# Attention's norms, maxima and denominators: from two-input VectorE steps to one-input sums over neighbouring columns

## The chip, the core and the metric

One Trainium2 chip, one of its cores. The time is the device time of one execution in microseconds (us), the median of several runs. The engines named below are TensorE (PE, with its weight loads PEld), VectorE (DVE), ScalarE (ACT), GpSimd (POOL) and SyncE (SP, which here only starts transfers). Each works through its own list of instructions in order and waits on semaphores for the others.

## The reference, cut to what matters

```python
# attention by random features; batch 4, heads 8, seq 576, head_dim 64, 128 features
q_s, k_s = q * 64**-0.25, k * 64**-0.25
def phi(x):
    proj = einsum('bhsd,md->bhsm', x, omega)
    sq = sum(x * x, -1) / 2.0
    h = proj - sq
    h = h - max(h, -1)
    return exp(h) / sqrt(128)
q_p, k_p = phi(q_s), phi(k_s)
kv = einsum('bhsm,bhsd->bhmd', k_p, v);  z = sum(k_p, 2)
num = einsum('bhsm,bhmd->bhsd', q_p, kv)
den = einsum('bhsm,bhm->bhs', q_p, z)[..., None] + 1e-06
x = num / den                       # (2304 tokens, 512)
# then a top-1 mixture of 8 experts (512 -> 1024 -> 512, ReLU), then an MLP 512 -> 2048 -> 512
```

In exact arithmetic `sq` drops out of `h - max(h)`. The kernel keeps it, so that its rounding follows the reference's.

## The kernel before, in words

The program has three stages: attention with the router (about the first 175 us), the experts, and the last MLP. The change touches the first alone.

Attention works on blocks of 256 tokens of one batch (or of 64 tokens of two batches), 20 for q and k together, and on 36 units: one unit is 4 pairs of heads of a block. For a block, its raw values are squared (`square`: ACT for k, POOL for q), POOL folds the 64 squares of a head into 16 (`tree`, two additions), and DVE sums the 16 (`total`, L449) into `nsq`, one number for each token and head. For a unit, PE transposes (L472), ACT copies (L477), PE projects (L484) into two PSUM banks, DVE takes the maximum over the features of each bank (`top`, L491, into `mx`), DVE forms the exponent's bias in two small steps on 128x8 numbers (`bias`: L495 writes mx = nsq * SQ + mx, L496 writes bi = nsq * SQ - mx, with SQ = -1/16), and ACT takes eight exponentials with that bias (`exps`, L500). k's exponentials go into the sums over tokens (L526), q's are transposed (L584), copied (L588 by ACT, L590 by DVE) and multiplied with those sums (L601). ACT copies the result, 73 columns a head, into `nx` (`copy_out`, L604): 64 numerators, 1 denominator, 8 router logits. DVE adds the epsilon to the denominator (`den`, L612), inverts it (L615), scales the logits (L618) and sums them over the heads (L622). The router's own steps on DVE follow (L657 to L691), and POOL scales the rows that are stored for the experts (L691, `xr`).

The order of the work on all engines is written by a planner (`Plan.run`): each step is added with an engine, a cost, a rank and what it comes after, and the planner's list is the order in which the instructions stand in each engine's queue. DVE and POOL are each one such queue: whatever is late there holds up all that stands behind it. DVE also carries work that belongs to the later stages, such as the second halves of the expert weights (`wl`, L290), and POOL the first halves (L281).

Of the kernel before, what the change touches and what calls it, by code (L numbers as in the profile page):

```python
# [8 lines left out]
F32 = mybir.dt.float32  # L9
# [4 lines left out]
AF = mybir.ActivationFunctionType  # L14
ALU = mybir.AluOpType
AX = mybir.AxisListType.X
# [3 lines left out]
P = 128  # L20
B, H, S, HD = 4, 8, 576, 64
# [6 lines left out]
HV = HD + 1  # L28
HZ = HD + 9
# [3 lines left out]
EPS = 1e-06 * 128.0  # L33
SCALE = float(HD) ** -0.25
SQ = -1.0 / 16.0
# [4 lines left out]
class Plan:  # L40
# [19 lines left out]
    def buf(self, ring):  # L60
        return {"ring": ring, "uses": 0, "end": 0.0}
# [100 lines left out]
def kernel(  # L162
# [14 lines left out]
    nc = tc.nc  # L177
# [146 lines left out]
    with ExitStack() as actx:  # L324
        ap = actx.enter_context(tc.tile_pool(name="ap", bufs=2))
# [3 lines left out]
        def ring(n, shape, name, dtype=F32, pool=ac):  # L329
            return [pool.tile(shape, dtype, name=f"{name}{i}") for i in range(n)]  # L330

        plan = Plan({
            "ps": ring(8, [P, 4, P], "ps", pool=psp),
            "blk": ring(7, [P, 2 * H, HD], "blk"),
            "sqt": ring(2, [P, 2 * H, HD], "sqt"),
            "th": ring(4, [P, 4, P], "th"),
            "pp": ring(11, [P, H, P], "pp"),
            "qt": ring(4, [P, 4, P], "qt"),
            "nx": ring(4, [P, H, HZ], "nx"),
            "xr": ring(3, [P, H, HD], "xr"),  # L340
            "kvc": ring(1, [P, 4, HD], "kvc"),
            "kvt": ring(1, [P, 2, P], "kvt"),
# [2 lines left out]
        add, buf, at = plan.add, plan.buf, plan.tile  # L345
# [11 lines left out]
            nc.gpsimd.memset(tv[:, :, HD:HV], 1.0)  # L357
        for t in kvz:
            nc.gpsimd.memset(t[:, H * HZ:], 0.0)

        def load_v(b):
            t = vmain[b % 2]
# [52 lines left out]
        dve, act, pool = nc.vector, nc.scalar, nc.gpsimd  # L415


        def block_tasks(which, blk, rank):
            src = q if which == "q" else k
            small = blk[0] == "s"  # L420
            n = H if small else 2 * H
            o = {"buf": buf("blk")}

            def load():
                t = at(o["buf"])
                if small:
                    for i in range(2):
                        nc.sync.dma_start(out=t[64 * i:64 * i + 64, 0:H, :],
                                          in_=src[2 * blk[1] + i, :, 512:576, :].rearrange("h p d -> p h d"))
                else:  # L430
                    b, i = blk
                    nc.sync.dma_start(out=t.rearrange("p (h r) d -> p h r d", r=2),
                                      in_=src[b, :, i * 256:(i + 1) * 256, :].rearrange("h (p r) d -> p h r d", r=2))

            def square(eng):
                raw, t = at(o["buf"])[:, 0:n, :], at(sb)[:, 0:n, :]
                if eng == "ACT":
                    act.activation(t, raw, AF.Square)
                else:
                    pool.tensor_mul(t, raw, raw)  # L440

            def tree():
                t = at(sb)[:, 0:n, :]
                for w in (32, 16):
                    pool.tensor_add(t[:, :, 0:w], t[:, :, 0:w], t[:, :, w:2 * w])

            def total():
                o["nsq"] = ap.tile([P, 2 * H], F32, name="nsq", tag="nsq", bufs=12)
                dve.reduce_sum(o["nsq"][:, 0:n], at(sb)[:, 0:n, 0:16], axis=AX)  # L449

            f = 0.5 if small else 1.0
            sb = buf("sqt")
            o["load"] = add("SP", 2250 * f, load, rank - 8, take=[o["buf"]])
            if which == "k":
                t = add("ACT", 950 * f, lambda: square("ACT"), rank - 0.5, after=[o["load"]], take=[sb], use=[o["buf"]])
            else:
                t = add("POOL", 1900 * f, lambda: square("POOL"), rank - 0.5, after=[o["load"]], take=[sb],
                        use=[o["buf"]])
            t = add("POOL", 2000 * f, tree, rank - 0.4, after=[t], use=[sb])
            o["sq"] = add("DVE", 60 + 270 * f, total, rank - 0.3, after=[t], use=[sb])  # L460
            return o

        def unit_tasks(u, o, rank, prev):
            which, blk, hf = u
            r = {}
            ptb, thb, ppb = buf("ps"), buf("th"), buf("pp")

            def turn():  # L470
                for c in range(4):
                    nc.tensor.transpose(at(ptb)[:, c, :],  # L472
                                        at(o["buf"]).rearrange("p a d -> p (a d)")[:, (4 * hf + c) * P:(4 * hf + c + 1) * P],
                                        ident)

            def copy():
                act.activation(at(thb), at(ptb), AF.Copy)  # L477

            def project(c):
                for w in HALVES:
                    for i in range(2):
                        nc.tensor.matmul(at(pjb[i])[w, c, :], lhsT=at(thb)[HALVES[i], c, w], rhs=oms[HALVES[i], :],  # L484
                                         start=True, stop=True)

            def top(i):
                if i == 0:
                    for name in ("mx", "bi"):
                        r[name] = ap.tile([P, 2, 4], F32, name=name, tag=name, bufs=6)  # L490
                dve.reduce_max(r["mx"][:, i, :], at(pjb[i]), axis=AX)  # L491

            def bias():
                sq = o["nsq"][:, 8 * hf:8 * hf + 8].rearrange("p (j i) -> p i j", i=2)
                dve.scalar_tensor_tensor(out=r["mx"], in0=sq, scalar=SQ, in1=r["mx"], op0=ALU.mult, op1=ALU.add)  # L495
                dve.scalar_tensor_tensor(out=r["bi"], in0=sq, scalar=SQ, in1=r["mx"], op0=ALU.mult, op1=ALU.subtract)  # L496

            def exps(i):
                for j in range(4):
                    act.activation(at(ppb)[:, 2 * j + i, :], at(pjb[i])[:, j, :], AF.Exp, bias=r["bi"][:, i, j:j + 1])  # L500

            pjb = [buf("ps"), buf("ps")]
            ta = add("PE", 435, turn, rank - 1.5, after=[o["load"]] + prev, take=[ptb], use=[o["buf"], ptb], mode="whole")
            x = add("ACT", 480, copy, rank - 2.4, after=[ta], take=[thb], use=[ptb])
            for c in range(4):
                x = add("PE", 220, lambda c=c: project(c), rank + 1 + 0.1 * c, after=[x, setup],
                        take=[] if c else pjb, use=[thb] + pjb, mode="quarters")
            ends, tb, t = [], x, x
            for i in range(2):
                t = add("DVE", 600, lambda i=i: top(i), rank + 4.5, after=[t], use=[pjb[i]])  # L510
            t = add("DVE", 150, bias, rank + 1, after=[t, o["sq"]])
            for i in range(2):
                ends.append(add("ACT", 1005, lambda i=i: exps(i), rank + 2, after=[t] + ends[0:1],
                                take=[ppb] if i == 0 else [], use=[pjb[i]]))
            return {"done": ends, "buf": ppb, "ta": ta, "tb": tb}
# [55 lines left out]
        def c_tasks(t, us, kvs, rank):  # L571
            it = tiles[t]
            r = {}
            ptb, qtb, nmb = [[buf(n), buf(n)] for n in ("ps", "qt", "ps")]
            nxb = r["buf"] = buf("nx")
# [25 lines left out]
                        nc.tensor.matmul(nm[w, h, 0:HZ], lhsT=qt[:, h, w], rhs=kz[i], start=True, stop=True)  # L601

            def copy_out(hf):
                act.activation(at(nxb)[:, 4 * hf:4 * hf + 4, :], at(nmb[hf])[:, :, 0:HZ], AF.Copy)  # L604
                if hf:
                    r["nx"] = at(nxb)
                    r["den"] = ap.tile([P, H, 1], F32, name="den", tag="den", bufs=10)
                    r["rden"] = ap.tile([P, H, 1], F32, name="rden", tag="rden", bufs=2)
                    r["lg"] = ap.tile([P, H, E], F32, name="lg", tag="lg", bufs=5)

            def den():
                dve.tensor_scalar_add(r["den"], r["nx"][:, :, HD:HV], EPS)  # L612

            def rec():
                dve.reciprocal(r["rden"], r["den"])  # L615
# [9 lines left out]
            bufs = [u["buf"] for u in us]  # L625
# [187 lines left out]
        for s, u in enumerate(units):  # L813
            which, blk, hf = u
# [21 lines left out]
            for us, b0, b1 in new:  # L836
                t = len(cts)
                kvs = [d for b in {b0, b1} for hf_ in range(2) for d in kvdone[b, hf_]]
                cts.append(c_tasks(t, us, kvs, s + 2 + 0.5 * len(new)))
                if t in groups:  # L840
                    t0, n = groups[t]
# [20 lines left out]
        n, key, at_, nums, off, offe = [small(f"t{i}", [P, E, 1]) for i in range(6)]  # L862
# [32 lines left out]
        for m in range(NB):  # L895
# [19 lines left out]
                                op0=ALU.logical_shift_right)  # L915
# [297 lines left out]
    with tc.If(tot > 0):  # L1213
        for t in ends:
            nc.sync.dma_start(out=sd[t * P:(t + 1) * P, :], in_=acc[t])
        for e in range(E):
# [4 lines left out]
            with tc.For_i(0, cnt_e, 1) as i:  # L1221
# [3 lines left out]
                for j in range(16):  # L1225
# [5 lines left out]
                    out=fx, out_offset=None, in_=xd,  # L1231
# [5 lines left out]
                for f in range(8):  # L1237
                    ph = ps_h2.tile([P, 512], F32, name="ph2", tag="ph2")[:, 0:P]
                    o = f % 2 * P
# [8 lines left out]
                for d in range(4):  # L1248
                    py = ps_h2.tile([P, 512], F32, name="ph2", tag="ph2")[:, 0:P]
                    o = d % 2 * P  # L1250
# [5 lines left out]
                for qd in range(4):  # L1256
# [3 lines left out]
                    for f in range(4):  # L1260
                        ph = ps_h2.tile([P, 512], F32, name="ph2", tag="ph2")[:, 0:P]
                        for d in range(4):
# [3 lines left out]
                                                op0=ALU.max, op1=ALU.min)  # L1266
# [9 lines left out]
                    out=out, out_offset=bass.IndirectOffsetOnAxis(ap=fu, axis=0), in_=fo, in_offset=None)  # L1276
# [36 lines left out]
```

## Time and profile before

| | us |
|---|---|
| median of 3 runs | 827.65 |
| lowest and highest of them | 824.15, 831.73 |
| the profiled execution | 828.41 |
| its span in the trace | 826.2 |

In the profile an engine's busy time counts from an instruction's start to its end, and an instruction that has started and is held up by something the semaphores don't show counts as busy too. A row of the timeline gives start, duration, engine, line, operation, output <- input with shapes, and in brackets the idle time ahead of it with what ended that. The chain of waits follows the end of the program back to its start, at each step to what was last.

### The profile page before, as it was taken

How to read it: one execution, taken by the hardware profiler on the slowest of the kernel's cores; microseconds unless marked ns; L12 is line 12 of the kernel's file. 1: busy time of each engine (PE TensorE's matmuls, PEld its weight loads, DVE VectorE, ACT ScalarE, POOL GpSimd, SP SyncE). 2: the span in 40 equal slices, each digit the busy share in tenths (PEclk: the TensorE clock that was granted, in tenths of full speed). 3: DMA queues.
4: the chain of work that ended last, by engine and by line, in shares of the span. 5: the costliest groups of instructions: out<-in, count | busy, mean ns of one | idle time of the engine just before them, and what ended most of it. 6: DMA issues, size and time to landing. Idle time of an engine off the chain costs nothing.

```text
span 826.2 us, 16881 instructions
## 1 busy us (share of the span) xinstructions
PE 778.4 (94%) x6530; PEld 710.1 (86%) x6530; DVE 570.1 (69%) x1124; ACT 366.9 (44%) x906; POOL 388.2 (47%) x385
## 2 busy tenths in 40 slices
PE   6798799769999999989999999999999999999996
PEld 4687688649999999979998989898999989898985
DVE  5679888865756876475688667687777877745543
ACT  6798799614422222222354554444433443434331
POOL 5627861444446455163655444453434544334333
PEclk9999999969999999999999999999999999999999
DMA  9958301155465655664432001110011100001112
GB/s 224 225 122 210 116 29 28 54 159 177 155 187 177 191 184 186 114 215 144 141 94 80 27 27 47 56 52 27 28 51 51 52 27 1 1 25 52 40 39 81
DMA packets 79034, 80.41 MB, mean 97 GB/s; under 512 B 28972, under 2 KB 61868, under 8 KB 78944
## 3 DMA queue, kind: packets, MB, share of 16 engines
q1 hardware_dynamic: 75056, 68.10, 29.2%
q0 software_dynamic: 3072, 9.57, 3.3%
q10 hardware_dynamic: 816, 1.57, 0.5%
q8 instruction: 53, 0.87, 0.4%
q14 instruction: 37, 0.30, 0.1%
HBM read 69.78 MB, written 9.45 MB: 96 GB/s over the span
## 4 chain that ended last, share of the span: by engine, by line
PE 71%; DVE 11%; DMA 8%; ACT 4%; issue 3%; POOL 2%; POOLq 0%; SPq 0%; DVEq 0%
PE ph L1117 7%; PE ph L1118 7%; PE ph L1119 7%; PE po L1163 7%; PE po L1162 7%; PE po L1161 7%; DMA out_dram<-acc,oidx 5%; PE py L1031 4%; PE py L1033 3%; PE py L1032 3%; PE ph L1013 3%; PE ph L1014 3%; PE ph L1015 3%; ACT pp L500 3%; DMA wraw<-in_moe_w_dram 2%
## 5 line engine op out<-in xcount | busy, mean ns | idle before, releaser
L1146 POOL TENSOR_TENSOR gl<-cl,gh 128x384 fp32r<-128x384 f32 x94 | 99.5, 1078 | 186.5 <-ACT gh L1145 186.5
L1138 ACT ACTIVATE cl<-cl,half 128x384 f32<-128x384 f32 x96 | 57.0, 615 | 212.4 <-DVE cl L1137 212.4
L1117 PE MATMUL ph<-yh,wh 128*128 128x384 f32 x384 | 129.8, 338 | 0.0
L1118 PE MATMUL ph<-yl,wh 128*128 128x384 f32 x384 | 129.7, 338 | 0.0
L1119 PE MATMUL ph<-yh,wl 128*128 128x384 f32 x384 | 129.7, 338 | 0.0
L281 POOL TENSOR_SCALAR wh<-wraw 128x1024 fp32r<-128x1024 f32 x60 | 75.0, 1252 | 111.9 <-DMA wraw<-in_moe_w_dram 46.8
L1163 PE MATMUL po<-wh,gl 128*128 128x512 f32 x288 | 113.9, 395 | 0.0
L1162 PE MATMUL po<-wl,gh 128*128 128x512 f32 x288 | 113.7, 395 | 0.0
L1161 PE MATMUL po<-wh,gh 128*128 128x512 f32 x288 | 113.6, 394 | 0.0
L1137 DVE TENSOR_SCALAR cl<-ph 128x384 f32<-128x384 f32 x96 | 51.4, 552 | 81.9 <-PE ph L1119 81.1
L290 DVE TENSOR_TENSOR wl<-wraw,wh 128x1024 fp32r<-128x1024 f32 x60 | 77.3, 1288 | 16.3 <-POOL wh L281 16.3
L500 ACT ACTIVATE pp<-ps,bi 128x128 f32<-128x128 f32 x288 | 84.3, 478 | 6.4 <-DVE bi L496 6.4
L937 DVE TENSOR_TENSOR yl<-yT,yh 128x384 fp32r<-128x384 f32 x96 | 79.0, 880 | 8.9 <-ACT yh L936 8.9
L1013 PE MATMUL ph<-xh,wh 128*128 128x288 f32 (+6 forms) x256 | 78.8, 308 | 3.0 <-DVE hl L1019 2.6
L1031 PE MATMUL py<-hh,wh 128*128 128x288 f32 (+6 forms) x256 | 79.1, 309 | 0.0
L1014 PE MATMUL ph<-xl,wh 128*128 128x288 f32 (+6 forms) x256 | 77.2, 302 | 1.1 <-DVE xl L975 1.0
L1032 PE MATMUL py<-hl,wh 128*128 128x288 f32 (+6 forms) x256 | 76.6, 299 | 0.7 <-DVE hl L1019 0.5
L1015 PE MATMUL ph<-xh,wl 128*128 128x288 f32 (+6 forms) x256 | 77.1, 301 | 0.0
L1033 PE MATMUL py<-hh,wl 128*128 128x288 f32 (+6 forms) x256 | 76.6, 299 | 0.4 <-DVE wl L290 0.4
L1117 PEld LDWEIGHTS ph<-yh,wh 128*128 128x128 f32 x384 | 72.1, 188 | 2.1
L1118 PEld LDWEIGHTS ph<-yl,wh 128*128 128x128 f32 x384 | 72.1, 188 | 2.0
L1119 PEld LDWEIGHTS ph<-yh,wl 128*128 128x128 f32 x384 | 72.1, 188 | 0.0
(163 smaller groups left out, 1664.6 us busy)
## 6 DMA issues: line engine op xcount, KB each, us to landing
wraw<-in_moe_w_dram SPq DMA_DIRECT2D x57, 512.0 KB, 3.8
wraw<-in_moe_w_in_dram SPq DMA_DIRECT2D x16, 512.0 KB, 3.9
wraw<-in_moe_w_out_dram SPq DMA_DIRECT2D x16, 512.0 KB, 3.4
blk<-in_k_dram SPq DMA_DIRECT2D x8, 512.0 KB, 6.6
blk<-in_q_dram SPq DMA_DIRECT2D x8, 512.0 KB, 6.1
vm<-in_v_dram SPq DMA_DIRECT2D x16, 256.0 KB, 5.3
xd<-xr SPq DMA_DIRECT2D x16, 256.0 KB, 2.2
wra<-in_moe_w_dram SPq DMA_DIRECT2D x4, 512.0 KB, 7.0
```

The lines of the kernel that those rows point to most:

```text
L500: act.activation(at(ppb)[:, 2 * j + i, :], at(pjb[i])[:, j, :], AF.Exp, bias=r["bi"][:, i, j:j + 1])
L1013: nc.tensor.matmul(ph, lhsT=wh[:, d, c], rhs=xh, start=(d == 0), stop=False)
L1014: nc.tensor.matmul(ph, lhsT=wh[:, d, c], rhs=xl, start=False, stop=False)
L1015: nc.tensor.matmul(ph, lhsT=wl[:, d, c], rhs=xh, start=False, stop=(d == 3))
L1031: nc.tensor.matmul(py, lhsT=wh[:, a, c], rhs=hh, start=(f == 0), stop=False)
L1032: nc.tensor.matmul(py, lhsT=wh[:, a, c], rhs=hl, start=False, stop=False)
L1117: nc.tensor.matmul(ph[f], lhsT=wh[:, a, c], rhs=yh, start=(d == 0), stop=False)
L1118: nc.tensor.matmul(ph[f], lhsT=wh[:, a, c], rhs=yl, start=False, stop=False)
L1119: nc.tensor.matmul(ph[f], lhsT=wl[:, a, c], rhs=yh, start=False, stop=(d == 3))
L1161: nc.tensor.matmul(po, lhsT=gh[:, c], rhs=wh[:, a, :], start=(f == 0), stop=False)
L1162: nc.tensor.matmul(po, lhsT=gh[:, c], rhs=wl[:, a, :], start=False, stop=False)
L1163: nc.tensor.matmul(po, lhsT=gl[:, c], rhs=wh[:, a, :], start=False, stop=(f == 3))
```

## The change

Where a DVE step had two tensors as inputs (L495, L496) or a tensor and a constant (L612), it becomes a sum along the last axis of one tensor, over two neighbouring columns. For this, the negated norm and the maximum are written next to each other: `nsq` has three columns a head (norm, maximum, and their negated sum). The first new sum writes -(column 0 + column 1) into column 2, the second writes column 0 + column 2 into `bi`. The denominator's epsilon stands in a 74th column of `nx`, written once at the start by POOL (four memsets), and the sum runs over columns 64 and 73. The factor 1/16 that L495 and L496 applied moves into the squares: for k into ACT's square (scale 0.25 ahead of squaring), for q into a new POOL multiplication at the end of `tree` (10 of them: 8 on 128x16x16, 2 on 128x8x16 numbers). The planner's costs and ranks are as they were, and PE, ACT, DVE and SP hold as many instructions as before.

```diff
@@ -336,7 +336,7 @@
             "th": ring(4, [P, 4, P], "th"),
             "pp": ring(11, [P, H, P], "pp"),
             "qt": ring(4, [P, 4, P], "qt"),
-            "nx": ring(4, [P, H, HZ], "nx"),
+            "nx": ring(4, [P, H, HZ + 1], "nx"),
             "xr": ring(3, [P, H, HD], "xr"),
             "kvc": ring(1, [P, 4, HD], "kvc"),
             "kvt": ring(1, [P, 2, P], "kvt"),
@@ -357,6 +357,8 @@
             nc.gpsimd.memset(tv[:, :, HD:HV], 1.0)
         for t in kvz:
             nc.gpsimd.memset(t[:, H * HZ:], 0.0)
+        for t in plan.tiles["nx"]:
+            nc.gpsimd.memset(t[:, :, HZ:HZ + 1], EPS)
 
         def load_v(b):
             t = vmain[b % 2]
@@ -435,7 +437,7 @@
             def square(eng):
                 raw, t = at(o["buf"])[:, 0:n, :], at(sb)[:, 0:n, :]
                 if eng == "ACT":
-                    act.activation(t, raw, AF.Square)
+                    act.activation(t, raw, AF.Square, scale=0.25)
                 else:
                     pool.tensor_mul(t, raw, raw)
 
@@ -443,10 +445,20 @@
                 t = at(sb)[:, 0:n, :]
                 for w in (32, 16):
                     pool.tensor_add(t[:, :, 0:w], t[:, :, 0:w], t[:, :, w:2 * w])
+                if which == "q":
+                    pool.tensor_scalar(out=t[:, :, 0:16], in0=t[:, :, 0:16], scalar1=-SQ, scalar2=1.0,
+                                       op0=ALU.mult, op1=ALU.mult)
+
+
+            def norms():
+                if "nsq" not in o:
+                    o["nsq"] = ap.tile([P, 2 * H, 3], F32, name="nsq", tag="nsq", bufs=12)
+                return o["nsq"]
 
             def total():
-                o["nsq"] = ap.tile([P, 2 * H], F32, name="nsq", tag="nsq", bufs=12)
-                dve.reduce_sum(o["nsq"][:, 0:n], at(sb)[:, 0:n, 0:16], axis=AX)
+                dve.reduce_sum(norms()[:, 0:n, 0], at(sb)[:, 0:n, 0:16], axis=AX, negate=True)
+
+            o["norms"] = norms
 
             f = 0.5 if small else 1.0
             sb = buf("sqt")
@@ -485,19 +497,19 @@
                                          start=True, stop=True)
 
             def top(i):
-                if i == 0:
-                    for name in ("mx", "bi"):
-                        r[name] = ap.tile([P, 2, 4], F32, name=name, tag=name, bufs=6)
-                dve.reduce_max(r["mx"][:, i, :], at(pjb[i]), axis=AX)
+                m = o["norms"]()[:, 8 * hf:8 * hf + 8, 1].rearrange("p (j i) -> p i j", i=2)
+                dve.reduce_max(m[:, i, :], at(pjb[i]), axis=AX)
+
 
             def bias():
-                sq = o["nsq"][:, 8 * hf:8 * hf + 8].rearrange("p (j i) -> p i j", i=2)
-                dve.scalar_tensor_tensor(out=r["mx"], in0=sq, scalar=SQ, in1=r["mx"], op0=ALU.mult, op1=ALU.add)
-                dve.scalar_tensor_tensor(out=r["bi"], in0=sq, scalar=SQ, in1=r["mx"], op0=ALU.mult, op1=ALU.subtract)
+                r["bi"] = ap.tile([P, 4, 2], F32, name="bi", tag="bi", bufs=6)
+                m = o["norms"]()[:, 8 * hf:8 * hf + 8, :]
+                dve.reduce_sum(m[:, :, 2], m[:, :, 0:2], axis=AX, negate=True)
+                dve.reduce_sum(r["bi"].rearrange("p j i -> p (j i)"), m[:, :, 0:3:2], axis=AX)
 
             def exps(i):
                 for j in range(4):
-                    act.activation(at(ppb)[:, 2 * j + i, :], at(pjb[i])[:, j, :], AF.Exp, bias=r["bi"][:, i, j:j + 1])
+                    act.activation(at(ppb)[:, 2 * j + i, :], at(pjb[i])[:, j, :], AF.Exp, bias=r["bi"][:, j, i:i + 1])
 
             pjb = [buf("ps"), buf("ps")]
             ta = add("PE", 435, turn, rank - 1.5, after=[o["load"]] + prev, take=[ptb], use=[o["buf"], ptb], mode="whole")
@@ -601,7 +613,7 @@
                         nc.tensor.matmul(nm[w, h, 0:HZ], lhsT=qt[:, h, w], rhs=kz[i], start=True, stop=True)
 
             def copy_out(hf):
-                act.activation(at(nxb)[:, 4 * hf:4 * hf + 4, :], at(nmb[hf])[:, :, 0:HZ], AF.Copy)
+                act.activation(at(nxb)[:, 4 * hf:4 * hf + 4, 0:HZ], at(nmb[hf])[:, :, 0:HZ], AF.Copy)
                 if hf:
                     r["nx"] = at(nxb)
                     r["den"] = ap.tile([P, H, 1], F32, name="den", tag="den", bufs=10)
@@ -609,7 +621,7 @@
                     r["lg"] = ap.tile([P, H, E], F32, name="lg", tag="lg", bufs=5)
 
             def den():
-                dve.tensor_scalar_add(r["den"], r["nx"][:, :, HD:HV], EPS)
+                dve.reduce_sum(r["den"][:, :, 0], r["nx"][:, :, HD:HZ + 1:HZ - HD], axis=AX)
 
             def rec():
                 dve.reciprocal(r["rden"], r["den"])
```

DVE, in the stretch of the second q blocks of batch 0; `nsq`, `mx`, `bi`, `den` are the tiles of the text above, `sqt` holds squares, `ps` is a PSUM bank, and the size is that of the output. Before:

```order
L495 SCALAR_TENSOR_TENSOR mx<-nsq,mx 128x8 [waits DVE_49]
L496 SCALAR_TENSOR_TENSOR bi<-nsq,mx 128x8 [waits DVE_49]
L449 TENSOR_REDUCE nsq<-sqt_117 128x16 [waits Pool_49]
L491 TENSOR_REDUCE mx<-ps_107 128x4
L612 TENSOR_SCALAR den<-nx_140 128x8 [waits Activation_49]
L615 RECIPROCAL rden<-den 128x8 [waits DVE_49]
L618 TENSOR_TENSOR lg<-nx_140,rden 128x64 [waits DVE_49]
L622 TENSOR_REDUCE lall<-lg 128x8 [waits DVE_49]
```

The same place with the change (between L501 and L624 a second pair of L507 and L508 stands, as there was a second pair of L495 and L496):

```order
L507 TENSOR_REDUCE nsq<-nsq 128x8 [waits DVE_49]
L508 TENSOR_REDUCE bi<-nsq 128x8 [waits DVE_49]
L459 TENSOR_REDUCE nsq<-sqt_117 128x16 [waits Pool_49]
L501 TENSOR_REDUCE nsq<-ps_107 128x4
L624 TENSOR_REDUCE den<-nx_140 128x8 [waits Activation_49]
L627 RECIPROCAL rden<-den 128x8 [waits DVE_49]
L630 TENSOR_TENSOR lg<-nx_140,rden 128x64 [waits DVE_49]
L634 TENSOR_REDUCE lall<-lg 128x8 [waits DVE_49]
```

The places in the queue and the semaphores waited on are the same, only the kind of instruction and the inputs are others.

POOL, at the same point of the program (the squares that the L449 or L459 above waits for are `sqt_117`). Before:

```order
L445 TENSOR_TENSOR sqt_117<-sqt_117 128x16x32
L445 TENSOR_TENSOR sqt_117<-sqt_117 128x16x16 [waits Pool_49]
L445 TENSOR_TENSOR sqt_118<-sqt_118 128x16x32 [waits Activation_49]
L445 TENSOR_TENSOR sqt_118<-sqt_118 128x16x16 [waits Pool_49]
L440 TENSOR_TENSOR sqt_117<-blk_115 128x512 [waits DMAHW5_49,DMAHW4_49,DVE_49]
```

With the change:

```order
L447 TENSOR_TENSOR sqt_117<-sqt_117 128x16x32
L447 TENSOR_TENSOR sqt_117<-sqt_117 128x16x16 [waits Pool_49]
L449 TENSOR_SCALAR sqt_117<-sqt_117 128x16x16 [waits Pool_49]
L447 TENSOR_TENSOR sqt_118<-sqt_118 128x16x32 [waits Activation_49]
L447 TENSOR_TENSOR sqt_118<-sqt_118 128x16x16 [waits Pool_49]
L442 TENSOR_TENSOR sqt_117<-blk_115 128x512 [waits DMAHW5_49,DMAHW4_49,DVE_49]
```

One instruction stands more in the queue, behind q's tree and ahead of the k tree that follows it.

## Rows read from the trace of the kernel before

**Rows 1.** Busy time by stretch: us, busy us (instructions) by engine, PE clock, DMA share, GB/s

```profile
38.00:62.00 24.00, 21.23 (x475) 18.61 (x474) 18.98 (x58) 21.33 (x70) 7.21 (x7) 0.99 0.64 133
62.00:82.00 20.00, 17.08 (x294) 14.63 (x294) 18.98 (x55) 17.51 (x57) 14.75 (x19) 0.91 0.85 216
82.00:100.00 18.00, 13.56 (x307) 12.12 (x307) 15.27 (x44) 12.04 (x40) 16.62 (x19) 0.91 0.41 119
100.00:125.00 25.00, 22.37 (x527) 19.82 (x526) 20.99 (x65) 23.27 (x77) 15.55 (x18) 1.00 0.09 34
125.00:153.00 28.00, 27.12 (x565) 24.68 (x563) 22.91 (x84) 26.50 (x92) 4.03 (x10) 1.00 0.08 22
153.00:172.00 19.00, 9.97 (x179) 7.95 (x179) 17.58 (x94) 6.27 (x19) 11.05 (x20) 0.72 0.28 103
```

**Rows 2.** Groups by line, shapes apart: busy us, mean ns, idle before

```profile
L445 POOL TENSOR_TENSOR sqt<-sqt 128x256 f32<-128x256 f32 x20 | 15.6, 780 | 2.5 <-ACT sqt L438 1.1
...
L496 DVE SCALAR_TENSOR_TENSOR bi<-nsq,mx 128x8 f32<-128x8 f32 x36 | 11.7, 325 | 1.2
...
L495 DVE SCALAR_TENSOR_TENSOR mx<-nsq,mx 128x8 f32<-128x8 f32 x36 | 10.8, 299 | 0.3
...
L612 DVE TENSOR_SCALAR den<-nx 128x8 f32<-128x8 f32 x18 | 7.7, 429 | 4.9 <-ACT nx L604 4.8
```

**Rows 3.** Single lines: duration ns minimum/median/maximum, first and last start, forms

```profile
L495 DVE SCALAR_TENSOR_TENSOR mx<-nsq,mx x36: 115/164/1593, 11.9 to 146.9; 128x8 f32<-128x8 f32 x36
...
L496 DVE SCALAR_TENSOR_TENSOR bi<-nsq,mx x36: 166/167/1214, 12.1 to 147.1; 128x8 f32<-128x8 f32 x36
...
L612 DVE TENSOR_SCALAR den<-nx x18: 118/168/1706, 58.9 to 166.1; 128x8 f32<-128x8 f32 x18
...
L449 DVE TENSOR_REDUCE nsq<-sqt x20: 274/408/420, 8.6 to 121.2; 128x16 f32<-128x256 f32 x16, 128x8 f32<-128x128 f32 x4
...
L667 DVE TENSOR_REDUCE rmm<-req x10: 152/166/170, 61.1 to 168.2; 128x2 f32<-128x16 f32 x8, 128x1 f32<-128x8 f32 x2
...
L622 DVE TENSOR_REDUCE lall<-lg x18: 252/268/273, 59.8 to 167.3; 128x8 f32<-128x64 f32 x18
...
L723 POOL TENSOR_SCALAR oa<-ohall,cs x36: 260/270/891, 65.1 to 170.5; 128x8 bf16<-128x8 bf16 x36
```

**Rows 4.** Timeline of POOL: start, us, engine, line, operation

```profile
6.56 2.06 POOL L445 TENSOR_TENSOR sqt<-sqt 128x512 f32<-128x512 f32 x2 [3.48 <-ACT sqt L438]
...
87.97 1.05 POOL L281 TENSOR_SCALAR wh<-wra 128x1024 fp32r<-128x1024 f32 x1
88.98 1.90 POOL L440 TENSOR_TENSOR sqt<-blk 128x1024 f32<-128x1024 f32 x1
90.96 5.10 POOL L445 TENSOR_TENSOR sqt<-sqt 128x512 f32<-128x512 f32 x4
...
163.62 2.06 POOL L691 TENSOR_TENSOR xr<-nx,den 128x512 f32<-128x512 f32 x2
```

**Rows 5.** Timeline of DVE at the same places

```profile
88.37 0.68 DVE L612 TENSOR_SCALAR den<-nx 128x8 f32<-128x8 f32 x1
...
89.20 1.71 DVE L612 TENSOR_SCALAR den<-nx 128x8 f32<-128x8 f32 x1
...
91.29 1.03 DVE L618 TENSOR_TENSOR lg<-nx,rden 128x64 f32<-128x64 f32 x1
...
164.97 0.79 DVE L618 TENSOR_TENSOR lg<-nx,rden 128x64 f32<-128x64 f32 x1
```

**Rows 6.** The chain of waits: start, us, what; first and last piece on the changed lines

```profile
38.60 1.13 DVE bi L496
...
163.99 0.72 DVE den L612
```

**Rows 7.** Waits of an engine from 38 to 153 us: us, times, longest

```profile
ACT pp L500 <- DVE bi L496: 6.1, 9, 1.2
...
DVE nsq L449 <- POOL sqt L445: 2.7, 2, 2.2
```

## The prediction

> **What bounds the kernel now.** I read the busy time by stretch first. Attention has no single bound: from 62 to 82 us DVE is busy 18.98 of 20 us, from 100 to 153 ACT and PE lead (ACT 23.27 of 25, PE 27.12 of 28), and from 153 to 172 DVE again with 17.58 of 19 [rows 1]. The reader should see how close the three run: an engine that gets faster soon meets another. Everything behind 175 us is untouched and starts when attention ends, so a microsecond gained at the end of attention is one of the whole.
>
> Next the groups by line. L495, L496 and L612 work on 8 numbers a partition, yet they take 299, 325 and 429 ns in the mean [rows 2]. One by one, their medians are 164, 167 and 168 ns and their maxima 1593, 1214 and 1706 ns [rows 3]. So most cost what any small step costs, and some are held up. Their busy time is 10.8 + 11.7 + 7.7 = 30.2 us; at the medians it would be 36 x 0.164 + 36 x 0.167 + 18 x 0.168 = 14.9 us. The **excess is 15.3 us**.
>
> What holds them up is seen in two timelines side by side. `den` starts at 88.37 and ends at 89.05, when POOL's L281 ends (87.97 + 1.05 = 89.02). The next `den` starts at 89.20 and ends at 90.91, when POOL's L440 ends (88.98 + 1.90 = 90.88) [rows 4, 5]. A DVE step that reads two SBUF tensors, or a tensor and a constant, starts while POOL works on an instruction and doesn't end before POOL's does. DVE's sums and maxima don't show it: L449, L667 and L622 have maxima of 420, 170 and 273 ns, a few ns above their medians, though L449 and L622 read SBUF amid POOL's work [rows 3].
>
> **The change, part by part.** *The 90 small steps become sums.* Price of one: the nearest rows are L667 (16 numbers in, 2 out, 166 ns) and L622 (64 in, 8 out, strided, 268 ns) [rows 3]. The new sums take 16 in and give 8. I take 0.166 us, since L667 agrees in what is read; that equals the medians of what it replaces, so the base price cancels. At L622's price they would cost 90 x 0.1 = 9 us more; that end is kept for the range. Below L667 nothing is in sight.
>
> *What of the excess lies on the path.* The chain of waits holds 15 pieces on L495, L496 and L612, between 38.60 and 163.99 us [rows 6]; together they are 10.9 us long. At 0.166 us each, 2.5 us would stay, so **8.4 us** of waiting is on the chain. The other 6.9 us of the excess lies beside ACT or PE, a part of it before 38 us, where the chain has no piece on these lines yet [rows 3, 6]; I count it as nothing, and if that cover went it would be a further gain.
>
> *What is handed on.* L618, the product with two tensors that stands two places behind `den`, still waits for POOL. Around 88 us: with sums, both `den` are done by about 88.9, the first L618 ends when L281 does, near 89.3, the second is ready near 89.7 and must wait for L440's end, 90.88; it ends near 91.1 where it ended at 91.29 + 1.03 = 92.32 [rows 4, 5]. 1.2 us is won of the 0.51 + 1.54 = 2.05 us that the two `den` waited. That takes off 0.85 us, and I take off 0.25 us for smaller cases: **-1.1 us**.
>
> *The end of the stage gives more than `den` shows.* POOL's pair of L691 from 163.62 is two of 1.03 us, ending at 164.65 and 165.68. Now `den` waits for the first and L618, behind it, for the second: it ends at 164.97 + 0.79 = 165.76. With sums, L618 is reached while the first still runs and ends near 164.9: 0.9 us won, where the chain counted 0.55 [rows 4 to 6]. The same pattern stands at 153.9 us. Together **+0.75 us**.
>
> *POOL's ten multiplications.* One has one input of 256 numbers (128 in two of them). Between L723 (8 numbers, 0.27 us) and L281 (1024, 1.05 us) the line gives 0.46 us; the bounds are 0.27 us and the 0.78 us of L445's two-input addition of that shape [rows 2 to 4]. Eight at 0.46 and two at 0.37 make 4.4 us on POOL. They count where DVE waits for q's squares: from 38 to 153 us it waits for POOL twice, 2.7 us in all [rows 7], once behind a q tree (0.46 us), and I count one more place where DVE, now earlier, comes before the tree is done: **-0.9 us**. What is queued behind L459 there is the whole of DVE, the next maxima and the next bias first.
>
> *The rest at nothing.* ACT's scale rides in the square that runs anyway. The four memsets come ahead of POOL's first wait, which is 3.48 us long [rows 4]; without it the first tree would wait for them. ACT's copies to `nx` now skip a column a head; at 10 ns more each, the 36 would cost 0.4 us of ACT.
>
> Sum: 8.4 - 1.1 + 0.75 - 0.9 = 7.15 us. From 38 to 62 and from 100 to 153 us ACT and PE have 1 to 3 us of idle time in each stretch [rows 1], so not all arrives: I take off another 1.1 us. **Gain 6.0 us.** The profiled execution is 828.41 us, 0.76 above the median of 827.65; against the median, 821.6 us.
>
> **The rivals.** *More than the chain shows (gain of 8.5 to 14 us).* ACT waits 6.1 us for the bias alone [rows 7], and a DVE that is held up less starts POOL's L691 and PE's projections earlier too. All 15.3 us less 0.9 us would give 813.2. For it: DVE's 95% from 62 to 82 us. Against it: the chain names 8.4 us and no more.
>
> *Handed on entirely (gain of 0 to 3 us, about 826).* Each wait that goes comes back at L618, at `wl` or at POOL's squares. For it: POOL is busy 14.75 of 20 and 16.62 of 18 us from 62 to 100 [rows 1]. Against it: after a bias, what follows on DVE is mostly a sum or a maximum from PSUM, which doesn't wait.
>
> *The sum of pairs is itself slow (gain near 1 us, 826.6).* At L622's 268 ns the 90 steps cost 9 us more, and with the share that lies on the chain (8.4 of 15.3) 5 us of the gain goes. It pays back in full only from 335 ns each (30.2 us by 90). The Trainium skill, page "VectorE: DVE Perf Modes", section "Rules for kernel authors", speaks for this side: it calls the reduction DVE's slowest operation, to be restructured away on a hot path. The trace disagrees at this size, by L667's 166 ns against 164 to 168 [rows 3]; only an output for every pair is not covered by a row.
>
> *Slower: POOL sets the pace from 62 to 125 us.* There POOL is at 47 of 63 us [rows 1] and seven of the ten multiplications fall in. At the upper price, 0.78 us for five and half of that for the two smaller, POOL's queue, with L691 and the next squares behind it, gets 4.7 us longer; DVE's sums over q's squares come that much later and DVE's gain becomes waiting. That gives 832.4, and 834.7 if the three others count too. It decides as soon as POOL's work between two waits for DVE exceeds DVE's own; the 2.2 us wait is such a place, and it is the only long one.
>
> *No effect at all*, if sums of SBUF pairs are held up by POOL like the rest: the maxima of L449 and L622 speak against it; 828.5, by the 0.9 us of POOL's work alone.
>
> **How the numbers follow.** Forecast (gain of 3 to 8.5 us) 0.50; more 0.26; handed on 0.10; slow sums 0.06; POOL 0.06; no effect 0.02. A measurement here tells about 1%, 8.3 us, from no change. Faster by more than that takes a gain above 8.3 us: 0.26 and 0.02 of the forecast, 0.28. Slower by as much needs the upper end of POOL's case and a slow sum besides: 0.04. Within 1%: 0.68. Most of the chance has one sign. The range goes from 814.5 (most of the excess gone) to 828.5 (all handed on), and leaves out 0.08 below and 0.1 above.
>
> **What would show it.** The lines that take the place of L495, L496 and L612 should have maxima below 0.2 us and 90 x 0.166 = 15 us busy. ACT's wait for the bias should fall from 6.1 us to under 3. POOL's new line should read about 0.46 us, and DVE's wait for POOL's squares rise from 2.7 us by 1 to 2. The next place to look is L618's line, whose mean should stay or rise. The prediction is wrong if the new sums have a long tail, if DVE's wait for POOL rises by more than 4 us, or if attention ends 8 us earlier although the chain held 8.4 us.

## The result, and the profile after

| | before | with the change |
|---|---|---|
| median of 10 runs, us | 828.41 | 820.72 |
| lowest and highest, us | 824.15, 832.44 | 816.62, 822.21 |
| span of the profiled execution, us | 826.2 | 818.3 |
| first matmul of the experts starts at, us | 180.74 | 173.49 |

The ratio is **0.9903**, 95% interval 0.9882 to 0.9923: 8.0 us less, 6.4 to 9.8 by the interval (the medians of the table are 7.7 us apart). A second measurement of the same kernel, beside three others, gave 0.9925 (0.9898 to 0.9952), 6.2 us less, 4.0 to 8.4 by the interval. The forecast gain of 6.0 us lies in the second interval and just below the first; its range, 814.5 to 828.5 us, holds both medians. In the profiled pair 7.25 of the 7.9 us between the two spans lie ahead of the experts.

The three groups that take the place of [rows 2], by line in the first 175 us (busy us, mean ns, idle before), with three of the other steps on DVE that read two tensors, or a tensor and a constant, and with POOL's new line:

```profile
L740 DVE TENSOR_SCALAR ob<-cs,rank 128x384 bf16<-128x384 f32 x18 | 9.9, 570 | 0.1
...
L630 DVE TENSOR_TENSOR lg<-nx,rden 128x64 f32<-128x64 f32 x18 | 7.9, 437 | 0.2
...
L290 DVE TENSOR_TENSOR wl<-wra,wh 128x1024 fp32r<-128x1024 f32 x4 | 6.1, 1533 | 0.0
L508 DVE TENSOR_REDUCE bi<-nsq 128x8 f32<-128x16 f32 x36 | 6.1, 170 | 1.2
L507 DVE TENSOR_REDUCE nsq<-nsq 128x8 f32<-128x16 f32 x36 | 5.8, 161 | 0.3
...
L449 POOL TENSOR_SCALAR sqt<-sqt 128x256 f32<-128x256 f32 x8 | 3.3, 406 | 0.7
...
L624 DVE TENSOR_REDUCE den<-nx 128x8 f32<-128x16 f32 x18 | 3.0, 166 | 5.0 <-ACT nx L616 4.9
...
L449 POOL TENSOR_SCALAR sqt<-sqt 128x128 f32<-128x128 f32 x2 | 0.6, 300 | 0.2
```

The 30.2 us of [rows 2] have become 6.1 + 5.8 + 3.0 = 14.9 us. Instruction by instruction (minimum, median, maximum in ns), against [rows 3]:

```profile
L507 DVE TENSOR_REDUCE nsq<-nsq x36: 118/160/173, 10.8 to 140.3; 128x8 f32<-128x16 f32 x36
...
L508 DVE TENSOR_REDUCE bi<-nsq x36: 169/170/171, 11.0 to 140.5; 128x8 f32<-128x16 f32 x36
...
L624 DVE TENSOR_REDUCE den<-nx x18: 127/172/182, 55.7 to 158.3; 128x8 f32<-128x16 f32 x18
```

The medians are those of the steps they replace; the maxima of 1593, 1214 and 1706 ns are gone. The reader should see that the whole difference is in the tail of the distribution, none in the typical instruction.

The two places of [rows 4, 5] stand for all of them. In the trace before, 23 of the 90 steps took over 60 ns more than the median of their line. Each of the 23 began while an instruction was under way on POOL and ended 10 to 33 ns behind the end of that instruction. The rule has exceptions: 36 of the 90 began while POOL was at work, and 4 of these ended before POOL did, 3 of them beside POOL's steps on 8 numbers. With the change, 53 of the 90 sums began while POOL was at work, and 47 ended before it.

The place that the prediction worked out, in the timelines of DVE and POOL after the change (start, us), against [rows 4, 5]:

```profile
83.67 0.42 DVE L459 TENSOR_REDUCE nsq<-sqt 128x16 f32<-128x256 f32 x1 [2.71 <-POOL sqt L449]
84.00 0.17 DVE L624 TENSOR_REDUCE den<-nx 128x8 f32<-128x16 f32 x1
...
84.33 0.13 DVE L624 TENSOR_REDUCE den<-nx 128x8 f32<-128x16 f32 x1
84.45 0.40 DVE L630 TENSOR_TENSOR lg<-nx,rden 128x64 f32<-128x64 f32 x1
...
85.10 1.61 DVE L630 TENSOR_TENSOR lg<-nx,rden 128x64 f32<-128x64 f32 x1
```

```profile
83.72 1.05 POOL L281 TENSOR_SCALAR wh<-wra 128x1024 fp32r<-128x1024 f32 x1
84.73 1.89 POOL L442 TENSOR_TENSOR sqt<-blk 128x1024 f32<-128x1024 f32 x1
```

Both `den` now run through while L281 works. The first product waits for L281's end (84.77), the second, from 85.10, for L442's (86.62) and ends at 86.71. So here the wait did go on to L630.

The busy time by stretch, columns as in [rows 1]:

```profile
38.00:62.00 24.00, 21.98 (x486) 19.34 (x482) 18.43 (x57) 23.14 (x77) 11.63 (x10) 1.00 0.55 141
62.00:82.00 20.00, 16.69 (x376) 14.34 (x378) 17.07 (x56) 18.96 (x62) 17.34 (x25) 1.00 0.76 219
82.00:100.00 18.00, 13.65 (x254) 12.64 (x250) 14.96 (x48) 12.15 (x36) 15.25 (x18) 0.81 0.36 105
100.00:125.00 25.00, 25.00 (x608) 22.87 (x606) 19.30 (x65) 24.41 (x83) 14.03 (x19) 1.00 0.07 24
```

The stretches hold somewhat later work now, but the bound has moved: from 62 to 82 us ACT (18.96 of 20) and POOL (17.34) are ahead of DVE (17.07, where it had 18.98), and from 100 to 125 us PE has no idle time left. The chain of waits shows the same; this is its part from 60 to 72 us:

```profile
60.02 2.03 POOL xr L703
62.05 1.18 POOL oa L735 x4
63.23 0.69 POOL sqt L447
63.99 1.70 POOL sqt L447 x2
65.75 0.74 POOL sqt L447
66.58 0.41 POOL sqt L449
...
71.58 0.31 POOL sqt L449
71.92 0.29 DVE nsq L459
```

Twelve us of the chain lie on POOL without a break, two of the new multiplications among them. In the chain before, the same stretch held PE's and DVE's steps, among them the longest piece that the bias has on it:

```profile
69.61 1.21 DVE bi L496
```

And the waits of ACT and DVE from 38 to 153 us, against [rows 7]:

```profile
ACT rex L688 <- DVE rd L672: 4.0, 3, 2.4
ACT pp L512 <- DVE bi L508: 2.6, 3, 1.0
```

```profile
DVE nsq L459 <- POOL sqt L449: 3.5, 3, 2.7
...
DVE nsq L459 <- POOL sqt L447: 0.5, 1, 0.5
```

ACT's wait for the bias fell from 6.1 to 2.6 us, DVE's wait for POOL's squares rose from 2.7 to 4.0 us.

### The profile page after: what moved, and what is told of

It reads as the page before. It is cut to its first block, busy times and chain, and to the rows that moved or that the text cites. A ratio compares the mean times of both kernels' runs of the same rounds, so it can differ in the third digit from the quotient of the medians.

```text
span 818.3 us, 16895 instructions
## 1 busy us (share of the span) xinstructions
PE 776.6 (95%) x6530; PEld 709.9 (87%) x6530; DVE 553.8 (68%) x1124; ACT 367.1 (45%) x906; POOL 397.6 (49%) x399
## 4 chain that ended last, share of the span: by engine, by line
PE 74%; DVE 8%; DMA 7%; ACT 5%; POOL 3%; issue 2%; POOLq 0%; SPq 0%; DVEq 0%; ACTq 0%
PE ph L1129 7%; PE ph L1130 7%; PE ph L1131 7%; PE po L1175 7%; PE po L1174 7%; PE po L1173 7%; DMA out_dram<-acc,oidx 5%; PE py L1043 4%; PE py L1044 4%; PE py L1045 4%; PE ph L1025 3%; PE ph L1026 3%; PE ph L1027 3%; ACT pp L512 3%; PE ps L496 2%
## 5 line engine op out<-in xcount | busy, mean ns | idle before, releaser
L1158 POOL TENSOR_TENSOR gl<-cl,gh 128x384 fp32r<-128x384 f32 x94 | 102.1, 1106 | 186.9 <-ACT gh L1157 182.2
L281 POOL TENSOR_SCALAR wh<-wraw 128x1024 fp32r<-128x1024 f32 x60 | 76.6, 1278 | 109.7 <-DMA wraw<-in_moe_w_dram 86.3
```

Source lines behind the costliest of these rows:

```text
L1158: rest.tensor_sub(gl, cl, gh.bitcast(F32))
```

## The experiments

All ratios are to the kernel before, with 95% intervals; us are worked out with that kernel's median in the same comparison.

**1. The bias alone.** The change, with the denominator as it was:

```diff
-                dve.reduce_sum(r["den"][:, :, 0], r["nx"][:, :, HD:HZ + 1:HZ - HD], axis=AX)
+                dve.tensor_scalar_add(r["den"], r["nx"][:, :, HD:HV], EPS)
```

> Only the bias is formed by sums of pairs (with the three-column norms, ACT's scale and POOL's ten multiplications); the denominator is a step with a tensor and a constant again. Theory (what goes is the waiting for POOL's running instruction): the bias lines held 10.6 of the 15.3 us of excess and half of the chain's 8.4 us, so a gain of 3 to 5 us, ratio 0.994 to 0.997, with L612's like still showing maxima over 1 us. Rival (the end of the stage alone counts, where only the denominator stands): gain under 1.5 us, ratio 0.998 to 1.001.

Measured: 0.9947 (0.9923 to 0.9971), 4.4 us less. The denominator's line kept its tail:

```profile
L622 DVE TENSOR_SCALAR den<-nx x18: 120/218/1705, 51.8 to 158.6; 128x8 f32<-128x8 f32 x18
```

**2. The denominator alone.** The kernel before, with the 74th column and the sum over two columns:

```diff
-                dve.tensor_scalar_add(r["den"], r["nx"][:, :, HD:HV], EPS)
+                dve.reduce_sum(r["den"][:, :, 0], r["nx"][:, :, HD:HZ + 1:HZ - HD], axis=AX)
```

> Only the denominator is a sum of two columns; norms, maxima and bias as in the kernel before, and no multiplication on POOL. Theory: 4.2 us of the chain's waiting and the 0.75 us at the end, nothing paid on POOL: a gain of 3.5 to 5 us, ratio 0.994 to 0.996. Rival (the end alone counts): the whole gain of the change, ratio 0.990. Rival (the wait is handed on to the product behind it): under 1 us, ratio 0.999 to 1.001, with the product's mean up from 418 ns to over 600.

Measured: 0.9956 (0.9934 to 0.9978), 3.6 us less, with the bias lines as long as ever:

```profile
L497 DVE SCALAR_TENSOR_TENSOR mx<-nsq,mx 128x8 f32<-128x8 f32 x36 | 14.1, 392 | 0.3
...
L498 DVE SCALAR_TENSOR_TENSOR bi<-nsq,mx 128x8 f32<-128x8 f32 x36 | 10.2, 284 | 1.2
...
L620 DVE TENSOR_TENSOR lg<-nx,rden 128x64 f32<-128x64 f32 x18 | 7.1, 395 | 0.2
```

The two halves give 0.9947 x 0.9956 = 0.9903, the ratio of the whole; each has an interval of 0.002 to either side, so that the agreement to the last digit is chance. Neither rival holds: the end of the stage isn't alone in counting, and over the stage the product behind the denominator didn't take its wait over (395 ns in the mean, 418 before).

**3. Two inputs again.** All of the change but the kind of step:

```diff
-                dve.reduce_sum(m[:, :, 2], m[:, :, 0:2], axis=AX, negate=True)
-                dve.reduce_sum(r["bi"].rearrange("p j i -> p (j i)"), m[:, :, 0:3:2], axis=AX)
+                dve.tensor_add(m[:, :, 2], m[:, :, 0], m[:, :, 1])
+                dve.tensor_sub(r["bi"].rearrange("p j i -> p (j i)"), m[:, :, 0], m[:, :, 2])
...
-                dve.reduce_sum(r["den"][:, :, 0], r["nx"][:, :, HD:HZ + 1:HZ - HD], axis=AX)
+                dve.tensor_add(r["den"], r["nx"][:, :, HD:HV], r["nx"][:, :, HZ:HZ + 1])
```

> The changed kernel with its layout, its moved scales and its POOL work, but each of the 90 sums is an addition or a subtraction of two SBUF tensors over the same columns. Theory (reading two SBUF streams is what waits for POOL): the excess is back, 15 us busy above 15, the gain is gone and POOL's multiplications stay: ratio 0.999 to 1.004. Rival (layout, the scale in the squares, or anything but the kind of step gives the gain): ratio 0.988 to 0.992, and no line with a long tail.

Measured: 1.0039 (1.0019 to 1.0059), 3.2 us more. The tail is back:

```profile
L507 DVE TENSOR_TENSOR nsq<-nsq x36: 119/171/1633, 11.3 to 146.9; 128x8 f32<-128x8 f32 x36
...
L508 DVE TENSOR_TENSOR bi<-nsq x36: 169/171/1180, 11.5 to 147.1; 128x8 f32<-128x8 f32 x36
...
L624 DVE TENSOR_TENSOR den<-nx x18: 118/196/1717, 57.1 to 165.1; 128x8 f32<-128x8 f32 x18
```

Same columns, same places in the queue, same POOL: the kind of step gives the whole gain. What is left of the change without it costs 3.2 us (1.6 to 4.9 by the interval). Which part of it costs that, the layout, ACT's scale, POOL's multiplications or the denominator with two tensors, was not separated.

**4. POOL quiet.** The kernel before, with its two-input steps, but POOL without squares and trees; ACT's squares are left out as well, and the norms are zeros that DVE writes.

```diff
-                    pool.tensor_mul(t, raw, raw)
...
-                    pool.tensor_add(t[:, :, 0:w], t[:, :, 0:w], t[:, :, w:2 * w])
...
-                dve.reduce_sum(o["nsq"][:, 0:n], at(sb)[:, 0:n, 0:16], axis=AX)
+                dve.memset(o["nsq"][:, 0:n], 0.0)
```

> The kernel before with its two-input steps for bias and denominator, but POOL's squares and trees and ACT's squares are left out; the norms are zeros, written by DVE in the place of the sums over squares. POOL still scales rows (17), makes its small products and splits four weights. Theory (the steps wait for POOL's running instruction): the 72 bias steps, which met squares and trees, fall from 10.6 us of excess to under 3, with medians as before; the denominators, which meet the scaled rows too, keep 1 to 3 of their 4.7 us. Time: ratio 0.980 to 0.990. Rival (two SBUF inputs are slow by themselves, or wait for DVE's own work): the excess of the bias steps stays above 7 us.

Measured: 0.9788 (0.9750 to 0.9827), more than expected of it. The steps themselves:

```profile
L489 DVE SCALAR_TENSOR_TENSOR mx<-nsq,mx x36: 115/161/1022, 11.0 to 132.0; 128x8 f32<-128x8 f32 x36
...
L490 DVE SCALAR_TENSOR_TENSOR bi<-nsq,mx x36: 166/167/204, 11.2 to 132.2; 128x8 f32<-128x8 f32 x36
...
L606 DVE TENSOR_SCALAR den<-nx x18: 119/167/703, 53.5 to 151.2; 128x8 f32<-128x8 f32 x18
```

Their groups are 7.4, 6.1 and 4.2 us busy: 1.7 us of excess for the bias (10.6 before) and 1.2 us for the denominator (4.7). The instructions are the same; what is gone beside them is POOL's squares and trees and ACT's ten squares. That it is POOL and not ACT shows in the 6 steps here that still took over 60 ns more than their median: each ended within 60 ns behind the end of a POOL instruction under which it had begun, like all 24 such steps of experiment 3. This makes both halves of the cause: a step with two SBUF tensors, or with a tensor and a constant, and an instruction under way on POOL. Why a tensor and a constant count like two tensors, no run shows.

**5. Without POOL's multiplications.** The three lines that multiply q's squares by 1/16 are taken out; q's norms stand without the factor, which cancels in the bias.

> The changed kernel without POOL's ten multiplications; q's norms stand without their factor 1/16, which cancels in the bias. The prediction put 0.9 us of the 4.4 us on the path. Theory: 0.5 to 2 us faster than the change, ratio 0.988 to 0.990. Rival (POOL sets the pace from 62 to 125 us): 3 us or more, ratio 0.984 to 0.987. Rival (all hidden): no difference, 0.990 to 0.991.

Measured: 0.9904 (0.9877 to 0.9930), no different from the change's 0.9903. That is the figure of the rival that all is hidden. The interval still holds the theory, and leaves out the rival in which POOL sets the pace.

**6. The change once more, and with each multiplication twice.** The second multiplies by 1.

> The changed kernel once more, beside the three below on one chip. Both theories on POOL's multiplications start from it: ratio 0.988 to 0.993.

> The changed kernel with a second multiplication (by 1) behind each of POOL's ten, 3.9 us more on POOL. Theory (nearly all of it lies in POOL's idle time): 0 to 1.5 us slower than the change, ratio 0.990 to 0.993. Rival (POOL sets the pace from 62 to 125 us, and the two terms of the prediction on it were too small): 2.5 to 4 us slower, ratio 0.993 to 0.996.

Measured side by side: 0.9925 (0.9898 to 0.9952) and 0.9939 (0.9915 to 0.9963). Ten multiplications more cost 1.2 us by the ratios and 2.0 us by the medians, within the intervals; by itself the ratio of 0.9939 lies in the rival's range, by its distance from the change beside it in the theory's. Ten fewer brought nothing. The prediction's 0.9 us fits both, but the intervals overlap too far to tell it from nothing, or from the 2.5 us or more that the rival asks for.

**7. Without norms.** Squares, trees, sums and the bias steps cancel in exact arithmetic; here they are left out, and the maximum writes the bias:

```diff
-                dve.reduce_max(m[:, i, :], at(pjb[i]), axis=AX)
+                dve.reduce_max(r["bi"].rearrange("p j i -> p i j")[:, i, :], at(pjb[i]), axis=AX, negate=True)
```

once with all other instructions in the old order, once with the planner told.

> Squares, trees, sums of squares and the two sums of the bias are left out (they cancel in exact arithmetic); the bias is the negated maximum, written by the maximum itself. All other instructions stand in the order of the changed kernel. Gone are about 20 us of DVE, 55 us of POOL and 10 us of ACT. If DVE and POOL still hold up the stage after the change, 6 to 12 us faster than the change, ratio 0.976 to 0.984. Rival (PE and ACT have become the bound): under 4 us, ratio 0.986 to 0.990.

> The same left out, and the planner knows it, so that the order of all engines is another. Theory: at least what the kernel with the old order gives and up to 5 us more, ratio 0.970 to 0.984. Rival (the planner's order fits worse, or the experts' weights then arrive late and give it back): no better than with the old order.

Measured: 0.9805 (0.9773 to 0.9836) and 0.9775 (0.9748 to 0.9802; median 809.76 us), the fastest version here. The work that was left out, on DVE, on POOL and in ACT's squares, still held some 10 us of the stage after the change (0.9925 to 0.9805); how much of it belongs to which engine is not shown. The two orders differ by less than their intervals. Remarkable beside experiment 4: the kernel with old order and no bias steps (0.9805) is no faster than the one with 72 of them on a quiet POOL (0.9788). Within the intervals, some 4 us to either side, the steps' own 12 us are for the greater part covered.

## Why the prediction was right, step by step

- **Price of a sum: right.** 0.166 us was taken by L667, 160 to 172 ns came out. An output for each pair costs nothing that shows, so the rival of the slow sum falls: on a quiet POOL the old step took 167 ns (experiment 4, L490), the sum takes 170 (L508). The rule of the Trainium skill (VectorE: DVE Perf Modes, Rules for kernel authors) that the reduction is DVE's slowest operation does not show at 16 numbers.
- **Excess: right.** 15.3 us forecast, 30.2 - 14.9 = 15.3 us found.
- **Share on the chain: fits, as far as the times can tell.** The pieces of the chain gave 4.2 us each for bias and denominator; with POOL's 0.9 us off the one, and 1.1 off and 0.75 on at the other, 3.3 and 3.85 us were due, 4.4 and 3.6 measured, with intervals of 2.4 to 6.4 and 1.8 to 5.5 us. The count of 15 pieces is short: the chain holds 49 on these lines, 14.7 us long together. The other 34 are 0.22 us long at most, so that the 8.4 us of waiting change little.
- **Handed on: right at the place worked out, too small over the stage.** From the start of the sum over squares to the end of the second product the place at 88 us took 92.32 - 88.04 = 4.28 us, now 86.71 - 83.67 = 3.04: 1.24 us won, 1.2 forecast. Over the stage, L618's line (L630 now) rose from 7.5 to 7.9 us and the one-hot step `ob` (L728, now L740) from 8.8 to 9.9 us; `wl` fell from 6.3 to 6.1. The router's small steps with two inputs (L660, L664, L670, L673) took 1.3 us more together. So some 2.6 of 15.3 us came back at other steps, where the prediction took off 1.1 us. How much of it lies on the path is shown only for the end of the stage, in the next point.
- **End of the stage: right up to the product, too high behind it.** From the start of `den` to the end of the product it was 1.77 us [rows 5, 6]; these rows of after give 158.01 - 157.26 = 0.75, 1.0 us less (0.9 forecast):

```profile
157.26 0.18 DVE L624 TENSOR_REDUCE den<-nx 128x8 f32<-128x16 f32 x1 [0.56 <-ACT nx L616]
...
157.71 0.30 DVE L630 TENSOR_TENSOR lg<-nx,rden 128x64 f32<-128x64 f32 x1
```

  The place at 153.9 us won 1.0 us in the same way. But the next step with two inputs, `ob`, then meets the same POOL pair. At 148.01 us it took 1.21 us where it had taken 0.41, and 0.2 us of that 1.0 was left behind it; at the end of the stage 0.7 us was left. Together 0.9 us arrived, about what the chain had counted at these two places (0.45 and 0.55 us). So the extra +0.75 us, the term that the prediction put on top, does not show: it was handed on once more.
- **POOL's multiplications: priced a little high.** 0.41 and 0.30 us each, 3.9 us in all against 4.4. The long wait behind a q tree grew from 2.2 to 2.71 us, as worked out; the waits together by 1.3 us. That they cost 0.9 us of the whole, experiments 5 and 6 neither show nor exclude.
- **The last correction, 1.1 us for ACT and PE without idle time: open.** Without it the forecast was 7.15 us; the two measurements are 8.0 and 6.2 us, and 7.15 lies in both intervals.
- **Slower by POOL: the mechanism is there, its price isn't.** POOL does lead from 60 to 72 us, but the gain isn't lost there: the first rows for the experts were stored 1.5 us earlier than before, the second 4.9 us earlier.

The pair of profiles agrees with the sum, 7.25 against 7.15 us, better than it should. DVE's queue has the same order in both, so that the gain can be read step by step. At the router's step L664, 60.94 us before and 57.89 with the change, it is 3.0 us; the chain had 1.4 us of waiting up to there. From there to the end of the stage (L670, 167.78 and 160.35 us) it grows by 4.4 us; the chain and the three corrections give 5.7 for this part. Too much early and too little late make the sum come out: that is luck.

Some of the early gain is not the change's. At 33 us PE stood still in both, waiting for nothing that the profile shows:

```profile
34.83 0.97 PE L484 MATMUL ps<-oms,th 64*64 64x128 f32 x16 [2.15 <-issue]
```

```profile
32.86 0.67 PE L496 MATMUL ps<-oms,th 64*64 64x128 f32 x16 [0.46 <-issue]
```

In eleven profiled executions of ten kernels this gap was 0.20 to 2.15 us: 2.09 with the multiplications twice, 0.44 with the old steps on a quiet POOL, 0.46 and 0.52 in the two executions of the change. It doesn't go with the kind of step; what sets it is open. Behind it the bias began at 38.40 us before and at 36.60 with the change. These 1.8 us are most of the 2.7 us by which ACT's exponentials start earlier at 37.0 us; the bias itself gives 1.

The second execution of the change began the experts at 170.95 us, 9.8 us earlier than the kernel before and 2.5 us earlier than the first. By the prediction's own sign, attention that ends 8 us earlier, this execution speaks against it. The 2.5 us lie ahead of the router's step above (55.43 us here); from there on it gained 4.5 us, as the first did. So the late part repeats in both executions, and the early part, of which the prediction counted little, differs between them.

## What to carry to other kernels

Where a short step's mean is twice its median, read the maxima and lay the other engines' timelines beside them: here the held-up steps ended when POOL's instruction ended, and no semaphore showed it. Such a wait goes when the step is put into a form that doesn't share, even if that form is no shorter by itself; price it by the pieces on the chain of waits, then ask which step behind it will meet the same neighbour, and the next one after that. And before polishing a step, ask whether it cancels: leaving the norms out was worth more than twice the change.

## What the runs showed of the hardware that was not expected

- The wait is for what is left of POOL's instruction, however small DVE's step, and it goes both ways. In the timeline after the change, `wl` on DVE starts while POOL works on L703, and both take longer than alone (DVE 1.21 us at 86.63, POOL's pair 2.05 us at 156.89):

```profile
77.64 1.76 DVE L290 TENSOR_TENSOR wl<-wra,wh 128x1024 fp32r<-128x1024 f32 x1
```

```profile
77.28 3.02 POOL L703 TENSOR_TENSOR xr<-nx,den 128x512 f32<-128x512 f32 x2
```

- PE's stand at 33 us was followed by a lower clock in one execution only. In the kernel before, after 2.15 us, the granted clock was 0.77 from 34 to 36 us and 0.50, the lower of the two levels, from 36 to 38 us. After 0.46 us, with the change, it stayed at 1.00, but so it did after 2.09 us (the multiplications twice) and 2.10 us (no norms, old order). So the length of this stand alone doesn't decide.
- A gain at the end of attention can be given back among the experts. Without the multiplications the first expert matmul started at 171.58 us, 1.9 us before that of the change, yet the span was 820.2 us against 818.3: from 330 to 370 us PE was busy 34.5 of 40 us there, 37.4 with the change. PE waits there 1.8 us for weights and 3.7 us for DVE's `xl` and `hl`. Whether this belongs to that kernel or to that one execution was not tried.
